# Top-32 attention with two expert layers on one core: the folds of the top-k read half of the scores from PSUM, the scores lose their factor of 1/8, and the order list is new

## The chip, the cores and the metric

One NeuronCore of a Trainium2 chip runs the whole program. The metric is the device time of one execution in microseconds (us). The kernel before was run three times.

## The reference

```python
def _attn_ref(q, k, v):                      # 2 batches, 8 heads, 576 rows, head size 64
    scores = (1.0 / np.sqrt(64)) * np.matmul(q, k.transpose(0, 1, 3, 2))
    kth = np.partition(scores, -32, axis=-1)[..., -32:-31]
    scores = np.where(scores >= kth, scores, -1e9)
    attn = np.exp(scores - np.max(scores, axis=-1, keepdims=True))
    attn = attn / (np.sum(attn, axis=-1, keepdims=True) + 1e-09)
    return np.matmul(attn, v)

def reference(...):
    x = attention output as (1152 tokens, 512)
    h = x @ w_in                             # 512 -> 2048
    x = (h * np.cos(h)) @ w_out              # 2048 -> 512
    # top-1 routing to 8 experts of width 1024 with capacity 288: relu(x @ w1[e]) @ w2[e], times the gate
```

All inputs and outputs are fp32. The softmax of each row of scores keeps the 32 largest of 576 values.

## The kernel before

**Attention.** The work is cut into 36 steps. 32 of them (kind "n", called whole steps here) take 128 query rows of one batch for a pair of heads; four of them (kind "s", steps 16, 17, 20 and 22) take the 64 rows left over in a batch for four heads. A step has 2 x 576 scores on each of the 128 partitions, `Sp[128, 2, 576]`. `scores(s, i)` computes them in two parts. Each part is four small matmuls into the PSUM tile `S` (two banks, one buffer in all), which ScalarE or VectorE then copies to `Sp` (`evict`, L820, profile lines L664 and L665) with a factor of 1/8. In a whole step, part i is column half i of both heads; in the other four, part i is both column halves of one pair of heads. `Sp` has four buffers.

**Top-k.** `pair_chain(s)` runs on VectorE (DVE). Two folds (L834) write the elementwise maximum of the two column halves of `Sp` into the first half of `C`, and the minimum into the second half. Then three rounds of `max` (the eight largest of 288, L839) and `match_replace` (L842) follow for each of two heads, and one `max` over all 576 columns of `C` (L846). `C` has a single buffer, so the folds of step s+1 come behind the chain of step s. `softmax(s)` then makes the threshold and the maximum into two biases (L873, on GpSimd, called POOL in the profile; `factors` holds the two factors), subtracts a penalty from all scores below the threshold (L880 on ScalarE, L884 on POOL or DVE), takes the exponential (L887) and divides by the sum (L897 to L899). `products(s)` transposes the result on TensorE (L914), evicts the transposed parts `PT` (L664 or L665) and multiplies by v (L928 to L943).

**What runs beside it.** While attention runs, the weights of the first layer arrive and are converted (`convert`, L691 to L711) and split in two (`split_w`, `split_wo`: `rounded` and `subtract`). As soon as a tile of 128 tokens is complete, `layer_in`, `cosine`, `product` and `layer_out` compute the first layer for it, and `route` and `place` send it to its expert. After the last tile the experts follow one behind the other.

**What sets the order.** Every operation is entered into a `Plan` with its engine, a cost and the tiles that it reads and writes. `PICKS` chooses the engine of each operation that could run on two or three (`flex`): one digit for each, in the order in which they are entered. `ORDER` lists the numbers of all operations; `in_order` takes them by that list, as soon as what they depend on has been issued, and issues each to its engine's queue. The queue of an engine runs strictly in that order, so a wait at its head holds all that is behind it. The cost numbers of the plan only choose which buffer of a ring is taken; they are no times of the chip.

The lines that the change touches:

```python
evict(0.53, 0.67, copy, r=[kp], w=[("Sp", s, i)], scale=0.125)                      # L820
DVE.tensor_tensor(out=T["C", s][:, :, c:c + HS], in0=x[:, :, 0:HS], in1=x[:, :, HS:S], op=op)   # L834
```

Of the kernel before, what the change touches and what calls it, by code (L numbers as in the profile page):

```python
# [19 lines left out]
HS = S // 2  # L20
# [26 lines left out]
    "1000000000010000000000000000000000000001000000000000000001000000000000000000000000000000000001001100"  # L47
    "1010000001100000010000000001010100000001000000000000000001100000000100000000000000000001001000010001"
    "0001000100002000000000000000002000000012000001000000000020000000000000000000000000000000000002000100"
    "1100110001111010111110110000000010000000000000000000000000010000001000010100100001001011110101000101"  # L50
    "0101111010000000010100000101010000000100000000000001010010111000010000000000000000000011010010010010"
    "0001010001100100000000001000001101011111101001000010001100000000000001010000001000000000111101001000"
    "000000000100")
ORDER = [
# [489 lines left out]
def forward(ctx, lasting, tc, kq, vn, vs_, w_in, w_out, w_gate, w1, w2, out, paired):  # L544
# [250 lines left out]
    def scores(s, i):  # L795
# [19 lines left out]
        def copy():  # L815
            x = T["Sp", s]
            o = x[:, :, i * HS:(i + 1) * HS] if kind == "n" else x[:, i, :].rearrange("p (a c) -> p a c", c=HS)
            return o, T[kp][:, :, 0:HS]
        P.op("pe", 0.595 if kind == "n" else 1.025, mm, r=[k], w=[kp], tiling="rows" if kind == "n" else "quarters")
        evict(0.53, 0.67, copy, r=[kp], w=[("Sp", s, i)], scale=0.125)  # L820

    def chain(s):
        if paired:
# [822 lines left out]
```

## Time and profile before

| | us |
|---|---|
| median of 3 runs (lowest, highest) | 654.29 (653.79, 655.72) |
| the profiled execution, time | 652.3 |
| the profiled execution, span from first to last instruction | 650.4 |
| busy in the span: TensorE (PE) | 580.4 |
| VectorE (DVE) | 556.5 |
| ScalarE (ACT) | 499.0 |
| GpSimd (POOL) | 311.2 |

A share of 89% for TensorE over the whole span hides that the stages differ: attention with its conversions fills the first 200 us, attention and the first layer share the next 200, the rest of the first layer runs to about 465 us, and the experts fill what remains. So the busy time has to be read by stretches.

### The profile page before, as it was taken

To read this page: it belongs to the slowest core of one execution; us is meant where nothing else is said; L and a number is where in the kernel's file an instruction comes from. 1 tells how busy PE (TensorE), PEld (TensorE's weight loads), DVE (VectorE), ACT (ScalarE), POOL (GpSimd) and SP (SyncE) were. 2 spreads that over 40 slices of the span, in tenths; PEclk is the share of its full clock that TensorE was granted. 3 is DMA by queue.
4 is the path that set the end of the run, shared out by engine and by line. 5 is a ranking of instruction groups with operands and counts; after the bars stand their busy time and mean duration, and the time that the engine had idled before them with its cause. 6 is when DMAs were issued, how large, how long until landed. Compare 5 with 4: busy or idle time off the path is not lost.

```text
span 650.4 us, 11538 instructions
## 1 busy us (share of the span) xinstructions
PE 580.4 (89%) x3808; PEld 452.7 (70%) x3808; DVE 556.5 (86%) x1542; ACT 499.0 (77%) x1026; POOL 311.2 (48%) x367
## 2 busy tenths in 40 slices
PE   3456589787989999999999999999979999999994
PEld 1234476565545876778767788788679898889893
DVE  6999999999999999999999989555666787878782
ACT  3688799989998978889998986636635777678771
POOL 2466776755875777854776633434341121010111
PEclk9986699898999999999999999999969999999998
DMA  8656597722252222233212210124444696668650
GB/s 290 228 172 210 162 389 282 236 88 62 60 146 84 85 79 83 66 104 99 74 44 66 78 42 18 66 98 145 148 147 145 221 292 206 203 214 269 222 181 17
DMA packets 44613, 94.62 MB, mean 145 GB/s; under 512 B 7165, under 2 KB 11261, under 8 KB 44544
## 3 DMA queue, kind: packets, MB, share of 16 engines
q1 hardware_dynamic: 42800, 89.04, 41.9%
q0 software_dynamic: 1744, 4.76, 2.0%
q8 instruction: 32, 0.52, 0.3%
q14 instruction: 37, 0.30, 0.1%
HBM read 81.87 MB, written 12.69 MB: 145 GB/s over the span
## 4 chain that ended last, share of the span: by engine, by line
PE 40%; DVE 33%; ACT 11%; issue 11%; DMA 2%; POOL 2%; SPq 0%; POOLq 0%; DVEq 0%; ACTq 0%
DVE C L842 8%; PE yp L1495 7%; DVE W L839 7%; DVE C L834 5%; PE x L1101 5%; PE hp L1450 4%; PE x L1093 4%; DVE W L846 3%; PE hp L1455 2%; ACT Sp L897 2%; PE av L928 2%; PE pt L914 2%; PE h L1013 2%; PE h L1018 2%; ACT Sp L887 2%
## 5 line engine op out<-in xcount | busy, mean ns | idle before, releaser
L884 POOL TENSOR_TENSOR Sp<-Sp,pen 128x576 f32<-128x576 f32 x60 | 81.7, 1362 | 42.9 <-ACT pen L880 39.7
L842 DVE MATCH_REPLACE8 C<-W,C 128x288 f32<-128x288 f32 x216 | 94.4, 441 | 0.0
L839 DVE MAX8 W<-C 128x8 f32<-128x288 f32 x216 | 92.7, 449 | 1.5
L1500 POOL DMA_INDIRECT out_dram<-ot,ti x16 | 18.9, 1179 | 136.9 <-DVE ot L1514 55.0
L914 PE MATMUL pt<-ident,Sp 128*128 128x128 f32 x324 | 54.7, 295 | 26.4 <-ACT Sp L897 21.2
L806 PE MATMUL S<-kq 64*128 64x288 f32 x256 | 57.6, 532 | 21.6 <-ACT Sp L664 12.2
L914 PEld LDWEIGHTS pt<-ident,Sp 128*128 128x128 f32 x324 | 38.6, 148 | 51.1 <-ACT Sp L897 29.4
L1093 PE MATMUL x<-wo,hs 128*128 128x512 f32 x148 | 72.5, 602 | 1.6 <-POOL wo L711 0.9
L834 DVE TENSOR_TENSOR C<-Sp 128x576 f32<-128x576 f32 x72 | 64.3, 899 | 1.2
L880 ACT ACTIVATE pen<-Sp,tb 128x576 bf16<-128x576 f32 x72 | 55.5, 771 | 8.6 <-POOL tb L873 4.4
L887 ACT ACTIVATE Sp<-Sp,tb 128x576 f32<-128x576 f32 x72 | 55.6, 773 | 5.2 <-DVE Sp L884 3.1
L1020 PE MATMUL h<-xh,wl 128*128 128x256 f32 x192 | 54.1, 282 | 0.0
L806 PEld LDWEIGHTS S<-kq 64*128 64x128 f32 x256 | 22.7, 216 | 43.7 <-ACT Sp L664 21.9
L928 PEld LDWEIGHTS av<-PT,v 128*64 128x64 f32 x320 | 38.5, 150 | 20.6 <-ACT ws L705 6.5
L928 PE MATMUL av<-PT,v 128*64 128x128 f32 x320 | 47.4, 301 | 6.0 <-DMA v<-in_vn_dram 2.9
L846 DVE MAX8 W<-C 128x8 f32<-128x576 f32 x72 | 52.3, 747 | 0.4
L664 ACT ACTIVATE PT<-pt 128x384 f32<-128x384 f32 x98 | 46.1, 486 | 6.8 <-PE pt L914 6.3
L897 ACT ACTIVATE Sp<-Sp,sm 128x576 f32<-128x576 f32 x55 | 41.0, 771 | 11.2 <-DVE sm L892 11.2
L930 PE MATMUL av<-PT,v 128*64 128x128 f32 x320 | 47.2, 301 | 0.3 <-ACT PT L664 0.3
L664 ACT ACTIVATE Sp<-S 128x576 f32<-128x576 f32 x62 | 40.1, 647 | 9.4 <-PE S L806 6.3
L1077 POOL TENSOR_TENSOR hs<-hs,ur 128x512 f32<-128x512 f32 x27 | 35.3, 1308 | 16.7 <-ACT ur L1068 16.6
L1455 PE MATMUL hp<-xgs,la 128*128 128x192 f32 (+2 forms) x160 | 39.8, 252 | 0.0
(224 smaller groups left out, 1863.0 us busy)
## 6 DMA issues: line engine op xcount, KB each, us to landing
raw<-in_w_dram SPq DMA_DIRECT2D x64, 512.0 KB, 4.5
kq<-in_kq_dram SPq DMA_DIRECT2D x40, 288.0 KB, 2.9
v<-in_vn_dram SPq DMA_DIRECT2D x32, 320.0 KB, 3.5
wraw<-in_w_in_dram SPq DMA_DIRECT2D x16, 512.0 KB, 4.7
wraw<-in_w_out_dram SPq DMA_DIRECT2D x16, 512.0 KB, 6.2
xs<-z SPq DMA_DIRECT2D x1, 4680.0 KB
v<-in_vs_dram SPq DMA_DIRECT2D x8, 320.0 KB
out_dram<-z SPq DMA_DIRECT2D x1, 2304.0 KB
```

Source lines behind the costliest of these rows:

```text
L664: P.flex([("act", act, lambda: ACT.activation(*args(), AF.Copy, scale=scale), False), ("dve", dve, lambda: DVE.tensor_scalar(*args(), scal ...
L806: PE.matmul(T[kp][:, a, 0:HS], t[p, S:S + 128], t[p, i * HS:(i + 1) * HS], start=True, stop=True)
L834: DVE.tensor_tensor(out=T["C", s][:, :, c:c + HS], in0=x[:, :, 0:HS], in1=x[:, :, HS:S], op=op)
L839: P.op("dve", 0.372, lambda r=r, i=i: DVE.max(T["W", s][:, i, LIST[r]:LIST[r] + 8], T["C", s][:, i, 0:HS]), r=[("C", s, i)], w=[("W", s, i)])
L842: P.op("dve", 0.42, lambda r=r, i=i: DVE.match_replace(T["C", s][:, i, 0:HS], T["W", s][:, i, LIST[r]:LIST[r] + 8], T["C", s][:, i, 0:HS], ...
L846: P.op("dve", 0.665, lambda i=i: DVE.max(T["W", s][:, i, 40:48], T["C", s][:, i, :]), r=[("C", s, i), ("C", s, 2)], w=[("W", s, i)])
L880: P.op("act", 0.67, lambda i=i, kp=kp: ACT.activation(T[kp], T["Sp", s][:, i, :], AF.Relu, scale=-BIG, bias=T["tb", s][:, i, 0:1]), r=[ks, ...
L884: eng.tensor_tensor(out=T["Sp", s][:, i, :], in0=T["Sp", s][:, i, :], in1=T[kp], op=OP.subtract)
L887: P.op("act", 0.76, lambda i=i: ACT.activation(T["Sp", s][:, i, :], T["Sp", s][:, i, :], AF.Exp, bias=T["tb", s][:, i, 1:2], accum_out=T[" ...
L914: PE.transpose(T[kp][:, c * 128:(c + 1) * 128], P2[:, cc * 128:(cc + 1) * 128], ident)
L928: PE.matmul(o[0:64, 0:128], v[:, c * 64:(c + 1) * 64], chunk(c), start=(c == 0), stop=(c == 4), skip_group_check=True)
L1093: P.op("pe", 0.87, lambda f=f, a=a: PE.matmul(T["x2", t], T[kh][:, a:a + 128], T["wo", f], start=(f == 0), stop=(f == 15)), r=[kh, ("wo", ...
```

## The change

The factor of 1/8 is taken out of the eviction of the scores. It moves into the exponential, whose scale becomes 0.125, and into the factor of the maximum's bias (-0.125 for -1). The folds take their second operand, the other column half, from the PSUM tile `S` instead of from `Sp`. In a whole step the two folds read part 1 of the scores in PSUM, both heads at once (128x576). In the other four steps there are four folds of 128x288, two for each part. So the folds no longer depend on the eviction of part 1, and part 1 stays in the single buffer of `S` until the folds and the eviction have read it. The last `max` depends on its own half of the minima alone. One cost of the plan changes (0.70 to 0.74), and `PICKS` and `ORDER` are new.

```
-                                    POOL.memset(factors[:, 1:2], -1.0)), w=[("halfpi",)])
+                                    POOL.memset(factors[:, 1:2], -0.125)), w=[("halfpi",)])
...
-        evict(0.53, 0.67, copy, r=[kp], w=[("Sp", s, i)], scale=0.125)
+        evict(0.53, 0.67, copy, r=[kp], w=[("Sp", s, i)])
...
-        both = [("Sp", s, 0), ("Sp", s, 1)]
-        firsts = [("C", s, 0), ("C", s, 1)]
-
-        def halves(c, op):
-            x = T["Sp", s]
-            DVE.tensor_tensor(out=T["C", s][:, :, c:c + HS], in0=x[:, :, 0:HS], in1=x[:, :, HS:S], op=op)
-        for c, op, w in ((0, OP.max, firsts), (HS, OP.min, [("C", s, 2)])):
-            P.op("dve", 0.67, lambda c=c, op=op: halves(c, op), r=both, w=w, port=True)
+        whole = steps[s][0] == "n"
+
+        def fold(c, op, i):
+            x, o = T["Sp", s], T["C", s]
+            if whole:
+                DVE.tensor_tensor(out=o[:, :, c:c + HS], in0=T["S", (s, 1)][:, :, 0:HS], in1=x[:, :, 0:HS], op=op)
+            else:
+                DVE.tensor_tensor(out=o[:, i, c:c + HS], in0=T["S", (s, i)][:, 1, 0:HS], in1=x[:, i, 0:HS], op=op)
+        if whole:
+            for c, op, w in ((0, OP.max, [("C", s, 0), ("C", s, 1)]), (HS, OP.min, [("C", s, 2), ("C", s, 3)])):
+                P.op("dve", 0.69, lambda c=c, op=op: fold(c, op, 0), r=[("Sp", s, 0), ("S", (s, 1))], w=w, port=False)
+        else:
+            for i in range(2):
+                for c, op, w in ((0, OP.max, ("C", s, i)), (HS, OP.min, ("C", s, 2 + i))):
+                    P.op("dve", 0.40, lambda c=c, op=op, i=i: fold(c, op, i), r=[("Sp", s, i), ("S", (s, i))], w=[w], port=False)
...
-                T["Sp", s][:, i, :], T["Sp", s][:, i, :], AF.Exp, bias=T["tb", s][:, i, 1:2],
+                T["Sp", s][:, i, :], T["Sp", s][:, i, :], AF.Exp, bias=T["tb", s][:, i, 1:2], scale=0.125,
...
-            P.op("pe", 0.70, mm, r=[gh, gl, ("vh", f), ("vl", f)], w=[("x2", t)])
+            P.op("pe", 0.74, mm, r=[gh, gl, ("vh", f), ("vl", f)], w=[("x2", t)])
```

What the new `PICKS` say, counted by reading its digits in the order in which the operations are entered (before -> after, up to the end of the first layer):

| operation | ACT | DVE | POOL |
|---|---|---|---|
| eviction of scores | 62 -> 66 | 10 -> 6 | |
| eviction of `PT` | 98 -> 89 | 10 -> 19 | |
| eviction of `h` | 31 -> 29 | 1 -> 3 | |
| penalty (L884) | | 12 -> 10 | 60 -> 62 |
| division (L897 to L899) | 55 -> 49 | 12 -> 10 | 5 -> 13 |
| scaling in `convert` (L691) | 31 -> 25 | | 1 -> 7 |
| `rounded` of w_in, w_out, gh | 31 -> 24 | | 13 -> 20 |
| `subtract` of the same | | 21 -> 13 | 23 -> 31 |
| clamp (L1047) | | 11 -> 8 | 25 -> 28 |
| product with the cosine (L1077) | | 9 -> 12 | 27 -> 24 |

In the weights of the first two experts, four more `rounded` and four more `subtract` go to POOL. What the new `ORDER` says of the tile `S`, read the same way: in 9 of the 32 whole steps the eviction of part 1 is issued before the two folds, in 15 between them, and in 8 behind both. In three of those 15 steps DVE has no other operation between the two folds, in twelve it has one or more.

## Rows read from the trace of the kernel before

**Rows 1.** Busy time by stretch: length, then busy us (instructions) of each engine, clock

```profile
core 0: us, PE busy (x) PEld busy (x) DVE busy (x) ACT busy (x) POOL busy (x), PEclk, DMA share, GB/s
0.00:200.00 200.00, 145.85 (x908) 94.34 (x909) 191.22 (x498) 169.02 (x318) 127.35 (x146) 0.91 0.57 190
200.00:400.00 200.00, 196.94 (x1434) 150.92 (x1433) 191.98 (x542) 174.36 (x331) 130.01 (x166) 1.00 0.24 72
400.00:465.00 65.00, 64.91 (x457) 53.16 (x457) 40.08 (x115) 37.21 (x70) 27.04 (x32) 1.00 0.29 98
465.00:650.40 185.40, 172.66 (x1016) 154.25 (x1014) 133.19 (x390) 118.41 (x309) 26.75 (x24) 0.96 0.59 193
```

**Rows 2.** Waits in 20 to 200 us: engine, line, releaser; us in total, times, longest

```profile
PE pt L914 <- ACT Sp L897: 20.3, 9, 6.8
```

**Rows 3.** DVE groups: line, operation, shapes, count; busy us, mean ns; idle before

```profile
L842 DVE MATCH_REPLACE8 C<-W,C 128x288 f32<-128x288 f32 x216 | 94.4, 441 | 0.0
L839 DVE MAX8 W<-C 128x8 f32<-128x288 f32 x216 | 92.7, 449 | 1.5
L834 DVE TENSOR_TENSOR C<-Sp 128x576 f32<-128x576 f32 x72 | 64.3, 899 | 1.2
L846 DVE MAX8 W<-C 128x8 f32<-128x576 f32 x72 | 52.3, 747 | 0.4
```

**Rows 4.** The folds' own line: durations min/median/max in ns, first and last start

```profile
L834 DVE TENSOR_TENSOR C<-Sp x72: 732/749/1827, 9.9 to 391.1; 128x576 f32<-128x576 f32 x72
```

**Rows 5.** Busy time of the folds alone, by stretch

```profile
0.00:200.00 200.00, 28.61 (x34) 0.91 0.57 190
200.00:395.00 195.00, 35.71 (x38) 1.00 0.24 74
```

**Rows 6.** Timeline of one slow fold: start us, us, engine, line, operation

```profile
65.42 1.28 POOL L884 TENSOR_TENSOR Sp<-Sp,pen 128x576 f32<-128x576 f32 x1
65.66 1.65 DVE L834 TENSOR_TENSOR C<-Sp 128x576 f32<-128x576 f32 x1
```

**Rows 7.** DVE instructions with an input in PSUM (first: min/median/max; others: groups)

```profile
L665 DVE TENSOR_SCALAR Sp<-S x10: 736/742/759, 5.3 to 388.2; 128x576 f32<-128x576 f32 x10
...
L1460 DVE TENSOR_TENSOR ht<-hp,ht 128x192 f32<-128x192 f32 x56 | 19.2, 351 | 9.2 <-ACT ht L1459 9.0
L1460 DVE TENSOR_TENSOR ht<-hp,ht 128x128 f32<-128x128 f32 x8 | 2.1, 286 | 2.7 <-ACT ht L1459 2.7
```

**Rows 8.** DVE groups whose counts the new picks change

```profile
L884 DVE TENSOR_TENSOR Sp<-Sp,pen 128x576 f32<-128x576 f32 x12 | 10.1, 838 | 1.1 <-ACT pen L880 1.1
L1077 DVE TENSOR_TENSOR hs<-hs,ur 128x512 f32<-128x512 f32 x9 | 8.6, 960 | 2.0 <-ACT ur L1068 1.9
L898 DVE TENSOR_SCALAR Sp<-Sp,sm 128x576 f32<-128x576 f32 x12 | 7.9, 673 | 0.2
L1047 DVE TENSOR_SCALAR ur<-hs 128x512 f32<-128x512 f32 x11 | 6.3, 581 | 0.3 <-ACT hs L664 0.2
L665 DVE TENSOR_SCALAR PT<-pt 128x384 f32<-128x384 f32 x10 | 5.5, 547 | 0.7 <-PE pt L914 0.7
L655 DVE TENSOR_TENSOR wl<-ws,wh 128x512 fp32r<-128x512 f32 x4 | 2.7, 674 | 0.0
L665 DVE TENSOR_SCALAR hs<-h 128x512 f32<-128x512 f32 x1 | 0.7, 684 | 0.0
```

**Rows 9.** Groups of ACT and POOL: the eviction of the scores, the penalty, the division

```profile
L664 ACT ACTIVATE Sp<-S 128x576 f32<-128x576 f32 x62 | 40.1, 647 | 9.4 <-PE S L806 6.3 <-PE pt L914 2.7 <-PE S L812 0.3
L884 POOL TENSOR_TENSOR Sp<-Sp,pen 128x576 f32<-128x576 f32 x60 | 81.7, 1362 | 42.9 <-ACT pen L880 39.7 <-PE pt L914 2.5
L899 POOL TENSOR_TENSOR Sp<-Sp,sm 128x576 f32<-128x576 f32 x5 | 6.1, 1213 | 1.7 <-DVE sm L892 1.7
```

**Rows 10.** Timeline of two hand-overs, DVE to ACT and ACT to PE

```profile
70.39 0.14 DVE L892 RECIPROCAL sm<-sm 128x2 f32<-128x2 f32 x1
...
70.56 1.44 ACT L897 ACTIVATE Sp<-Sp,sm 128x576 f32<-128x576 f32 x2 [1.43 <-DVE sm L892]
...
72.06 0.47 PE L914 MATMUL pt<-ident,Sp 128*128 128x128 f32 x1 [6.83 <-ACT Sp L897]
```

**Rows 11.** Timeline of four matmuls of one part of the scores

```profile
63.89 1.33 PE L806 MATMUL S<-kq 64*128 64x288 f32 x4
```

More of the change, by code (lines that the diff above doesn't have):

```diff
@@ L46 @@
 PICKS = (
[L47 to L53, printed above, removed]
-ORDER = [
[185 rows of a table removed]
+    "1000000000000000000000000000000010000000000000000200000000000000000000000000000110000100000001000100"
+    "0010000000010000000000000100000000010100000000000100000002000000000210000000001001000010000000100000"
+    "0000000000000000000022000100000110000002000000022000000022010000001000000010000001122000000010000101"
+    "0011110001201110111111110000001010010000010000000101100000000000000000000010110101111101110100100101"
+    "0101100000000111011101111101010000001000000000000000100110110111010000000110000000101001001000011011"
+    "0001010000010101001011100100100110001111111101001010000000000101101000000010110101110011110110010001"
+    "000000000000")
+ORDER = [
[186 rows of a table added]
 ]
@@ L845, in pair_chain @@
         for i in range(2):
-            P.op("dve", 0.665, lambda i=i: DVE.max(T["W", s][:, i, 40:48], T["C", s][:, i, :]), r=[("C", s, i), ("C", s, 2)],
-                 w=[("W", s, i)])
+            P.op("dve", 0.665, lambda i=i: DVE.max(T["W", s][:, i, 40:48], T["C", s][:, i, :]),
+                 r=[("C", s, i), ("C", s, 2 + i)], w=[("W", s, i)])
     def full_chain(s):
```

371 rows, old and new, of the table ORDER are left out of this document.

## Prediction

> **What bounds the kernel now.** I read the busy time by stretches first, since the share over the whole span mixes stages. In the first 200 us VectorE (DVE) is busy for 191 us, ScalarE (ACT) for 169 us and TensorE (PE) for only 146 us. From 200 to 400 us DVE has 192 us and PE 197 us, and from 400 to 465 us PE has no gap left [rows 1]. So DVE sets the pace for 200 us, both share it for the next 200 us, and from there on PE has a backlog that it works off. The waits confirm the first part: the longest wait of PE in that time, 20.3 us, is for ACT's division, the end of a softmax that waits for DVE's chain [rows 2]. The groups of DVE say what it does: the top-k lines sum to 304 us, and none of them stood idle for more than 1.5 us before its instructions [rows 3]. DVE is never short of scores.
>
> The folds differ from their neighbours. They take 0.749 us in the median and 0.732 us at best, but 1.83 us at worst and 0.899 us in the mean [rows 3, 4]. The timeline shows a slow one: it starts while POOL subtracts a penalty, and ends some 0.6 us after POOL is done, so that nearly all of its surplus lies beside POOL's instruction [rows 6]. All 72 folds lose 64.3 - 72 x 0.749 = 10.4 us in this way. Only 28.6 - 34 x 0.749 = 3.1 us of it falls in the first 200 us [rows 5], where DVE alone sets the pace.
>
> **The change part by part.** *The fold itself.* A DVE instruction with one input in PSUM shows no such spread: the eviction of 128x576 takes 0.736 to 0.759 us over ten instances, beside a POOL that is busy for two thirds of the time [rows 1, 7]. A tensor-tensor operation with one input in PSUM takes 0.286 us for 128 columns and 0.351 us for 192, so 1.02 ns for each column, which makes 0.351 + 384 x 0.00102 = 0.74 us for 576 [rows 7]. I take 0.745 us; the bounds are 0.73 and 0.76. Whole steps: 64 x (0.899 - 0.745) = 9.9 us less DVE time. The other four steps trade 8 folds of 0.899 us for 16 of 0.351 + 96 x 0.00102 = 0.45 us, which is nothing.
>
> [...]
>
> *The factor of 1/8.* Eviction, bias and exponential keep their number and sizes; a scale of an instruction that already has one or can take one costs nothing, bounded by the 0.647 us of the eviction, which already carries the factor [rows 9].
>
> *The new picks.* Until the end of the chain of step 17 (before, this was at about 197 us) the new list gives DVE 3 evictions of scores, 2 products, 3 clamps, 3 penalties and 5 subtractions fewer, and 1 division, 2 evictions of `PT` and 1 of `h` more. By the rows: -2.2 - 1.9 - 1.7 - 2.5 - 3.4 + 0.7 + 1.1 + 0.7 = -9.2 us [rows 7, 8]. The means of penalty, product, division and clamp hold waits beside POOL, which more POOL work brings back, so I take -7. Over the whole first layer it is only -4.0 us (4 x 0.742 + 2 x 0.838 + 2 x 0.673 + 8 x 0.674 + 3 x 0.581 - 9 x 0.547 - 2 x 0.684 - 3 x 0.960), as later steps get the evictions. ACT loses 26 instructions, at most 26 x 0.647 = 17 us [rows 9], which it can use at 169 of 200 us [rows 1]. POOL gains 31, at up to 1.36 us each 42 us at most, on 257 us in 400 us [rows 1, 9]; it stays below 80%, and its cover is that a step's softmax may lag by several steps, with four buffers of `Sp`.
>
> *The new hold on `S`.* Part 1 now stays in the one buffer until the folds have read it, so PE's scores of step s+1, and all that is queued on PE behind them, wait for the folds of step s; before, they waited for an eviction only. From there to the folds of s+1, DVE has the chain, 6 x (0.449 + 0.441) + 2 x 0.747 = 6.8 us [rows 3]. In that time PE and ACT need two parts and an eviction: at most 2 x 1.33 + 0.65 us plus hand-overs, 3.5 us [rows 9, 11]. A hand-over takes 0.03 to 0.06 us (70.53 to 70.56, 72.00 to 72.06) [rows 10]. So 3 us of slack hide this hold, if PE is not behind by more than that; it is no longer hidden by scores made steps ahead, and each us beyond the slack is one of DVE's.
>
> *The two readers of part 1.* ACT's eviction and DVE's folds now read the same PSUM tile. No row of before shows two engines reading one PSUM tile without an order between them. I assume that the reads are put one behind the other, in the order of issue. In the 15 whole steps where the eviction is issued between the folds, ACT then waits for the first fold, and the second fold, with all of DVE behind it, waits for ACT: 0.65 us and two hand-overs, 0.75 us, less what DVE has between the folds. With ACT free at once this leaves 0.75 us in three steps and 0 to 0.4 us in the others, some 3.5 us in all, 2 of it in the 8 such steps of the first 200 us; the bounds are 0 (the reads need no order) and 15 x 0.75 = 11 us. I take 3 us in the first 200 us, as ACT has a queue.
>
> **The sum.** At 200 us DVE is ahead by 10.1 us (folds 3.1, picks 7) less 3 us of waits, so by 7 us, and PE, with 54 us of gaps there, can follow. From 200 to 465 us PE has 465 - 200 - 196.9 - 64.9 = 3.2 us of gaps [rows 1]: what DVE saves there, another 7 us on the folds less some 3 us that the picks give back and 3 us of waits, has nowhere to go. For PE waiting at `S` I take off 1 us. That leaves 6 us. The experts (185 us) are the same work. So the span goes from 650.4 to 644.4 us; the profiled execution took 1.9 us more than its span, and the median of the runs is 2.0 us above the profiled execution: 648.3 us. With 0 to 8 us of waits instead of 3, and a PE that loses 0 to 2 us, the forecast's own range is 643.5 to 652.
>
> **The rivals.**
> *More gain.* No waits, and PE also closes its 3.2 us after 200 us: 10.1 + 3.2 = 13 us, 641 us. For it: three engines are relieved where two of them are full. Against: the 15 interleaved steps.
> *Nothing.* The gaps of PE before 200 us are those of a start that waits for conversions and softmax latencies, and PE is the bound after it. What DVE saves becomes idle time: 652.5 to 656. For it: most of the fold's surplus lies after 200 us [rows 5]. Against: DVE's 191 of 200 us.
> *The fold costs what it did.* If an input in PSUM costs more than rows 7 say, the folds save 5 us less, only some 1 us of it before 200 us; or the eviction delays every fold as before. That ends near 651.
> *Slower.* The hand-over of `S` decides: the second fold waits for ACT, the next scores wait for both, and the slack of the steps doesn't hold because DVE, PE and ACT are all nearly full. At 0.75 us for each of the 32 whole steps this costs 24 us, against 14.4 us that DVE saves over the layer (10.4 + 4.0): 9.6 us slower, 664 us. It decides from 14.4 / 32 = 0.45 us a whole step on. For it: 15 interleaved steps, and a list that shows no room for it in three of them. Against: 3 us of slack a step, and in 9 steps the eviction comes first, as it always did. [...]
>
> **How the numbers follow.** A measurement of this kernel can tell some 0.3% from no change, 2 us: faster is below 652.3, slower above 656.3. Forecast 0.47, more gain 0.13, nothing 0.16, the same fold 0.04, slower 0.20. Faster: 0.47 + 0.13 + 0.03 of the others = 0.63; same 0.16; slower 0.21. The range goes from 641 to 660: below lie 0.06 of the gain, above about half of the slower case and more.
>
> **What would show it.** Right: folds of 0.74 to 0.76 us with no long ones; DVE 10 to 17 us less busy before 465 us; waits of DVE's folds for ACT's eviction of 2 to 6 us in all; the first fold of step 18 at about 190 us; PE as full as before from there. Wrong: waits of the folds above 12 us, waits of PE's scores for the folds above 5 us, or PE gaps after 200 us. The prediction fails if the new list brings waits between other engines that no count of instructions shows.

## The result and the profile after

The changed kernel takes 664.16 us (median of 4 runs, 662.63 to 665.48) against 654.62 us for the kernel before on the same chip: a ratio of 1.0144, interval 1.0117 to 1.0171. That is 9.4 us slower (0.0144 x 655), where 6 us faster had been forecast. Below, "over before" is always such a ratio less 1, times 655 us, since each group of runs has its own runs of the kernel before (medians 654.6 to 655.6). The profiled execution has a span of 662.4 us, 12.0 us more than before, as the profiled execution of the kernel before, 652.3 us, lies 2.3 us below that median.

The busy time by stretches of the kernel after; it answers to [rows 1]:

```profile
core 0: us, PE busy (x) PEld busy (x) DVE busy (x) ACT busy (x) POOL busy (x), PEclk, DMA share, GB/s
0.00:200.00 200.00, 143.25 (x917) 92.91 (x918) 187.29 (x495) 163.34 (x307) 132.42 (x169) 0.93 0.56 186
200.00:400.00 200.00, 194.01 (x1393) 146.38 (x1392) 189.74 (x540) 167.60 (x315) 128.44 (x171) 1.00 0.25 77
400.00:465.00 65.00, 64.67 (x467) 53.99 (x466) 40.95 (x107) 32.95 (x63) 25.12 (x34) 1.00 0.26 89
```

Every busy share before 400 us is lower except POOL's in the first row. DVE is 5.3 us less busy until 465 us (423.3 to 418.0), ACT some 17 us less, and PE has done 5.5 us less by 400 us: three relieved engines and a longer run, so they wait for one another.

Cut at the same piece of work, the end of the last chain and the end of the first layer (its last matmul), the kernel before, then the kernel after:

```profile
0.00:406.30 406.30, 349.09 (x2395) 250.70 (x2396) 389.28 (x1058) 347.25 (x655) 259.77 (x313) 0.96 0.40 130
406.30:470.60 64.30, 64.21 (x426) 52.08 (x424) 37.08 (x101) 35.44 (x66) 24.64 (x30) 1.00 0.33 110
```

```profile
0.00:406.90 406.90, 344.16 (x2371) 245.56 (x2373) 382.79 (x1054) 335.26 (x629) 263.87 (x343) 0.97 0.40 129
406.90:480.70 73.80, 70.01 (x453) 55.48 (x448) 44.07 (x103) 32.78 (x63) 30.82 (x40) 0.98 0.30 104
```

The last chain ends only 0.6 us later: DVE has 6.5 us less work up to there, and 7.1 us more idle time. The layer ends 10.1 us later, and by PE: it stood idle for 62.7 instead of 57.2 us up to the last chain, and for 3.8 instead of 0.1 us behind it.

The groups of DVE, by shape (operation, shapes, count; busy us, mean ns; idle before). The first two answer to [rows 3, 4], the rest to [rows 8]:

```profile
L835 DVE TENSOR_TENSOR C<-S,Sp 128x576 f32<-128x576 f32 x64 | 47.5, 750 | 6.4 <-ACT Sp L665 4.4 <-PE S L807 0.3
L837 DVE TENSOR_TENSOR C<-S,Sp 128x288 f32<-128x288 f32 x16 | 6.8, 449 | 0.6 <-ACT Sp L665 0.4
...
L709 DVE SCALAR_TENSOR_TENSOR wt<-wraw,wt 128x512 int32<-128x512 int32 x29 | 23.2, 810 | 0.0
...
L892 DVE TENSOR_TENSOR Sp<-Sp,pen 128x576 f32<-128x576 f32 x10 | 10.5, 1052 | 0.7 <-ACT pen L888 0.7
L906 DVE TENSOR_SCALAR Sp<-Sp,sm 128x576 f32<-128x576 f32 x10 | 9.5, 950 | 0.1
L656 DVE TENSOR_TENSOR gl<-hs,gh 128x512 fp32r<-128x512 f32 x8 | 7.1, 886 | 5.0 <-POOL gh L661 3.2 <-ACT gh L660 1.8
```

The folds cost what was forecast, with no long ones left. Other operations of DVE got dearer: the penalty rose from 838 to 1052 ns, the division from 673 to 950 [rows 8]. The conversion, and the last subtraction, in the kernel before:

```profile
L708 DVE SCALAR_TENSOR_TENSOR wt<-wraw,wt 128x512 int32<-128x512 int32 x29 | 20.4, 714 | 0.0
L655 DVE TENSOR_TENSOR gl<-hs,gh 128x512 fp32r<-128x512 f32 x10 | 7.1, 715 | 0.8 <-ACT gh L659 0.7
```

Waits at the tile `S` in the whole span of the kernel after (engine, line, releaser: us, times, longest):

```profile
PE S L807 <- DVE C L835: 16.5, 4, 7.4
...
PE S L807 <- ACT Sp L665: 5.0, 6, 1.2
DVE C L835 <- ACT Sp L665: 4.4, 11, 0.7
...
ACT Sp L665 <- DVE C L835: 3.5, 6, 1.1
```

PE waits for the folds, and DVE and ACT take turns at part 1. The timeline shows the first at its longest. Scores from 10 us on, kernel before, then kernel after (start us, us, engine, line; in brackets the idle time before and what ended it):

```profile
13.10 1.33 PE L806 MATMUL S<-kq 64*128 64x288 f32 x4 [0.74 <-ACT Sp L664]
15.18 1.33 PE L806 MATMUL S<-kq 64*128 64x288 f32 x4 [0.75 <-ACT Sp L664]
```

```profile
14.83 1.33 PE L807 MATMUL S<-kq 64*128 64x288 f32 x4 [7.38 <-DVE C L835]
16.90 1.33 PE L807 MATMUL S<-kq 64*128 64x288 f32 x4 [0.74 <-ACT Sp L665]
25.45 1.33 PE L807 MATMUL S<-kq 64*128 64x288 f32 x4 [7.22 <-DVE C L835]
```

Before, PE ran ahead at the pace of the evictions; now it makes two parts and stands until the next folds. The same step 9, later in the run, before and after:

```profile
100.07 0.76 PE L806 MATMUL S<-kq 64*128 64x288 f32 x4
103.09 0.64 ACT L664 ACTIVATE Sp<-S 128x576 f32<-128x576 f32 x1
106.86 0.75 DVE L834 TENSOR_TENSOR C<-Sp 128x576 f32<-128x576 f32 x1
```

```profile
106.94 0.76 PE L807 MATMUL S<-kq 64*128 64x288 f32 x4
107.80 0.64 ACT L665 ACTIVATE Sp<-S 128x576 f32<-128x576 f32 x1
108.47 0.76 DVE L835 TENSOR_TENSOR C<-S,Sp 128x576 f32<-128x576 f32 x1 [0.45 <-ACT Sp L665]
```

The scores were done 106.86 - 100.83 = 6.0 us before their fold, now 108.47 - 107.70 = 0.8 us. Worked out in this way for the 31 whole steps from step 1 on (first fold's start less the modelled end of part 1's last matmul), the median of this lead fell from 6.0 to 1.0 us, and the steps with less than 1.9 us went from 2 to 21.

Near the end of the first layer a third thing shows. DVE, POOL and PE of the kernel after:

```profile
470.69 3.96 DVE L1237 TENSOR_TENSOR doubtb<-doubts 128x1 bf16<-128x1 f32 x1
474.58 0.68 DVE L1085 TENSOR_TENSOR hs<-hs,ur 128x512 f32<-128x512 f32 x1
...
470.87 3.77 POOL L657 TENSOR_TENSOR wl<-raw,wk 128x512 fp32r<-128x512 f32 x3
...
476.05 0.50 PE L1109 MATMUL x<-vh,gh 128*128 128x512 f32 x1 [2.98 <-ACT gh L660]
```

An addition of 128x1 takes 3.96 us beside three subtractions of POOL; behind it on DVE stands the product that PE's last matmuls need. After the 2.98 us in which PE stood, its granted clock, 1.00 until then, was 0.50 from 476.4 to 479.8 us, and its matmuls came 0.43 us apart instead of 0.23: some 1.6 us more for eight of them. (After 3.00 us in h2 it stayed at 1.00; and in the kernel before it was 0.50 from 475 to 485 us, behind 4.2 us in which PE's longest wait was 0.58 us.) Four us of these matmuls, and four us of them in the run f4 below, where PE did not wait so long:

```profile
476.00:480.00 4.00, 3.95 (x10) 2.90 (x11) 1.30 (x2) 0.00 (x0) 0.00 (x0) 0.57 0.36 123
```

```profile
474.00:478.00 4.00, 4.00 (x19) 3.21 (x18) 3.22 (x6) 0.63 (x1) 0.57 (x2) 1.00 0.26 67
```

The addition in the kernel before:

```profile
464.74 0.17 DVE L1229 TENSOR_TENSOR doubtb<-doubts 128x1 bf16<-128x1 f32 x1
```

The last matmul of the first layer ends at 480.7 us instead of 470.6 us (after, then before); what follows takes 181.7 and 179.8 us:

```profile
480.35 0.39 PE L1109 MATMUL x<-vh,gl 128*128 128x512 f32 x1
```

```profile
470.24 0.39 PE L1101 MATMUL x<-vh,gl 128*128 128x512 f32 x1
```

### The profile page after: what moved, and what is told of

It reads as the page before. It is cut to its first block, busy times and chain, and to the rows that moved or that the text cites. A ratio compares the mean times of both kernels' runs of the same rounds, so it can differ in the third digit from the quotient of the medians.

```text
span 662.4 us, 11583 instructions
## 1 busy us (share of the span) xinstructions
PE 583.6 (88%) x3808; PEld 452.8 (68%) x3808; DVE 557.3 (84%) x1541; ACT 484.3 (73%) x996; POOL 318.1 (48%) x406
## 4 chain that ended last, share of the span: by engine, by line
PE 41%; DVE 35%; issue 12%; ACT 6%; POOL 3%; DMA 1%; POOLq 0%; SPq 0%; DVEq 0%; ACTq 0%
DVE C L850 8%; DVE W L847 7%; PE yp L1503 6%; PE x L1109 5%; DVE C L835 4%; PE hp L1458 4%; PE x L1101 4%; DVE W L854 3%; PE h L1026 3%; DVE wt L709 3%; PE h L1028 2%; PE h L1027 2%; PE hp L1463 2%; PE av L936 2%; PE pt L922 2%
## 5 line engine op out<-in xcount | busy, mean ns | idle before, releaser
L807 PE MATMUL S<-kq 64*128 64x288 f32 x256 | 56.0, 519 | 33.4 <-DVE C L835 16.5
L1508 POOL DMA_INDIRECT out_dram<-ot,ti x16 | 16.1, 1004 | 140.1 <-ACT ot L1517 72.3
L1028 PE MATMUL h<-xh,wl 128*128 128x256 f32 x192 | 54.2, 282 | 0.0
L665 ACT ACTIVATE Sp<-S 128x576 f32<-128x576 f32 x66 | 42.3, 641 | 14.7 <-PE S L807 9.3
L835 DVE TENSOR_TENSOR C<-S,Sp 128x576 f32<-128x576 f32 x64 | 47.5, 750 | 6.4 <-ACT Sp L665 4.4
L665 ACT ACTIVATE PT<-pt 128x384 f32<-128x384 f32 x89 | 41.6, 488 | 13.7 <-PE pt L922 10.7
L936 PE MATMUL av<-PT,v 128*64 128x128 f32 x320 | 45.6, 291 | 5.5 <-DVE xl L969 4.0
L936 PEld LDWEIGHTS av<-PT,v 128*64 128x64 f32 x320 | 36.5, 144 | 17.9 <-DVE xl L969 5.5
L938 PE MATMUL av<-PT,v 128*64 128x128 f32 x320 | 45.6, 291 | 1.8 <-DVE PT L666 1.2
L905 ACT ACTIVATE Sp<-Sp,sm 128x576 f32<-128x576 f32 x49 | 37.0, 769 | 4.8 <-DVE sm L900 4.6
L1458 PE MATMUL hp<-xgs,wk 128*128 128x384 f32 x128 | 39.9, 374 | 0.0
```

What stands on the lines that cost most here:

```text
L665: P.flex([("act", act, lambda: ACT.activation(*args(), AF.Copy, scale=scale), False), ("dve", dve, lambda: DVE.tensor_scalar(*args(), scal ...
L807: PE.matmul(T[kp][:, a, 0:HS], t[p, S:S + 128], t[p, i * HS:(i + 1) * HS], start=True, stop=True)
L835: DVE.tensor_tensor(out=o[:, :, c:c + HS], in0=T["S", (s, 1)][:, :, 0:HS], in1=x[:, :, 0:HS], op=op)
L936: PE.matmul(o[0:64, 0:128], v[:, c * 64:(c + 1) * 64], chunk(c), start=(c == 0), stop=(c == 4), skip_group_check=True)
L1028: PE.matmul(o, lo, a, start=False, stop=(kc == 3), skip_group_check=True)
L1458: PE.matmul(o, hi_at(ka)[:, c:c + 128], x.rearrange("p a n -> p (a n)"), start=(kc == 0), stop=False, skip_group_check=True)
```

## The experiments

| run | us | ratio to before (95%) | over before, us |
|---|---|---|---|
| the change | 664.16 | 1.0144 (1.0117, 1.0171) | +9.4 |
| e1: folds from `S`, old lists | 729.97 | 1.1159 (1.1113, 1.1204) | +75.9 |
| e2: folds from `Sp`, new lists | 729.37 | 1.1144 (1.1100, 1.1188) | +74.9 |
| e3: eviction ahead of both folds | 670.68 | 1.0251 (1.0210, 1.0293) | +16.4 |
| e4: eviction behind both folds | 667.86 | 1.0189 (1.0144, 1.0234) | +12.4 |
| e5: new order, old picks | 671.71 | 1.0255 (1.0203, 1.0306) | +16.7 |
| f1: one reader of part 1 | 660.13 | 1.0074 (1.0050, 1.0098) | +4.8 |
| f4: three subtractions to DVE | 660.86 | 1.0079 (1.0050, 1.0108) | +5.2 |
| g4: f1 and f4 | 656.65 | 1.0023 (1.0001, 1.0045) | +1.5 |
| g1: before, shorter last maximum | 651.43 | 0.9937 (0.9905, 0.9968) | -4.1 |
| g2: after, shorter last maximum | 658.84 | 1.0051 (1.0030, 1.0073) | +3.3 |
| g3: factor of 1/8 alone | 654.27 | 0.9982 (0.9959, 1.0005) | -1.2 |
| h1: `S` held 0.8 us longer | 671.82 | 1.0234 (1.0185, 1.0284) | +15.3 |
| h2: no hold, new lists | 677.50 | 1.0365 (1.0330, 1.0400) | +23.9 |
| h3: h2 and a shorter last maximum | 665.22 | 1.0158 (1.0117, 1.0199) | +10.3 |
| h4: the folds of h2, old lists | 654.28 | 0.9976 (0.9952, 1.0001) | -1.6 |
| k1: h3, scores moved ahead | 735.24 | 1.1216 (1.1161, 1.1272) | +79.6 |
| k2: h4, scores moved back | 686.23 | 1.0475 (1.0439, 1.0512) | +31.1 |

The intervals reach 1.4 to 3.6 us to either side, so a difference of two rows is good to some 2 to 5 us.

**First question: the folds or the lists (e1, e2)?** e1 is the kernel after with the `PICKS` of before and its `ORDER`, 86 entries of it moved so that the scores of a step come behind the folds of the step before. e2 keeps the new lists:

```diff
-                DVE.tensor_tensor(out=o[:, :, c:c + HS], in0=T["S", (s, 1)][:, :, 0:HS], in1=x[:, :, 0:HS], op=op)
+                DVE.tensor_tensor(out=o[:, :, c:c + HS], in0=x[:, :, 0:HS], in1=x[:, :, HS:S], op=op)
```

> The changed kernel with the old PICKS and the old ORDER. The old list makes scores steps ahead, which the one buffer of S no longer allows: 86 of its entries (scores and their evictions) are moved to right behind the folds of the step before; in all 32 whole steps the eviction is issued ahead of the folds. Theory 1 (reading the folds from PSUM costs the time, by holding S and by ordering ACT and DVE): 659 us or more. Theory 2 (the new list and picks cost it, and the folds alone gain what they lose beside POOL): 648 to 653 us. Either way the folds take 0.745 us.

> The changed kernel with new PICKS and ORDER, but the folds read both halves from SBUF again, so that S is free after the eviction and ACT and DVE have no order on S. Theory 1 (PSUM read costs the time): 652 to 656 us, the waits of DVE's folds for ACT and of PE's scores for the folds go, the folds take 0.85 to 0.9 us again. Theory 2 (new list and picks): 663 to 668 us, since it loses the shorter folds and keeps the list.

Both came out at 729 to 730 us. By its letter e1 fits theory 1 ("659 us or more"), but e2, which takes the PSUM folds out, fits neither theory and is as slow. The longest waits at the scores, e1 first, then e2:

```profile
ACT Sp L663 <- PE S L805: 60.3, 36, 7.4
```

```profile
DVE C L835 <- ACT Sp L665: 38.6, 25, 3.4
```

Folds and lists can't be told apart by exchanging one of them: a list is made for one set of waits, and the new one has 23 of the 32 evictions of part 1 behind a fold that, in e2, must wait for them.

**Where the eviction stands between the folds (e3, e4).** In `ORDER`, the eviction of part 1 was moved in whole steps, here in step 5 (folds 228 and 229, eviction 227), in e3 and in e4:

```diff
-    164, 228, 201, 227, 169, 170, 229, 165,
+    164, 227, 228, 201, 169, 170, 229, 165,
```

```diff
-    164, 228, 201, 227, 169, 170, 229, 165,
+    164, 228, 201, 169, 170, 229, 227, 165,
```

> The changed kernel, with one edit of ORDER: in every whole step the eviction of part 1 is issued ahead of both folds (the change does so in 9 of 32). If the eviction between the folds is what costs time (4.4 us of DVE waits for it), 657 to 660 us. If not, 662 to 666 us.

> The changed kernel, with one edit of ORDER: in every whole step the eviction of part 1 is issued behind both folds. DVE then never waits for ACT at a fold of a whole step (4.4 us to 0), ACT waits for DVE and S is held longer. If DVE's waits for the eviction are the cause: 657 to 660 us. If the hold of S or ACT's queue counts more: 664 to 670 us. If the list as a whole is the cause: 662 to 666 us.

Both are dearer than the change's own mix, by 7.0 and 3.0 us, the second hardly clear of the noise. Neither place beats the one between the folds, so that place is not what costs.

**One reader (f1).**

```diff
-            return o, T[kp][:, :, 0:HS]
+            return o, x[:, :, 0:HS] if other else T[kp][:, :, 0:HS]
+        other = kind == "n" and i == 1
...
-        evict(0.53, 0.67, copy, r=[kp], w=[("Sp", s, i)])
+        evict(0.53, 0.67, copy, r=[("Sp", s, 0)] if other else [kp], w=[("Sp", s, i)])
```

> The changed kernel, but in the 32 whole steps the eviction of part 1 reads part 0 of Sp in SBUF instead of the PSUM tile S. So part 1 of S has one reader, the two folds, and neither engine waits for the other at it. Left out: part 1 of the scores never reaches Sp, so the softmax of these steps works on a copy of part 0; the top-k itself sees the right scores. Theory 'two readers' (ACT and DVE take turns at part 1 of S, and this is where the 10 us of the first layer go): 650 to 656 us, and the wait of DVE's folds for ACT's eviction (4.4 us) goes. Theory 'hold' (part 1 stays in the only buffer of S until the folds, whoever else reads it): 660 to 665 us.

4.6 us of the 9.4 went (4.0 by the medians). 660.1 us lies at the lower end of what the theory of the hold gave, and falls short of the 8 us or more that the theory of the two readers asked for: the second reader is a cause, not the whole. (In f1 the eviction doesn't wait for PE's part 1 either, but ACT's waits for scores fell from 9.3 to 7.7 us only.) The folds keep their 748 ns and no longer stand idle for ACT; the eviction from SBUF takes 675 ns:

```profile
L836 DVE TENSOR_TENSOR C<-S,Sp 128x576 f32<-128x576 f32 x64 | 47.1, 748 | 3.4 <-PE S L807 1.5
...
L665 ACT ACTIVATE Sp<-Sp 128x576 f32<-128x576 f32 x31 | 20.9, 675 | 0.0
```

A sibling of it (f2) freed `S` by folding part 0 with itself. Its values set off the kernel's own guard, which repeats the whole forward pass, so its 1438 us can't be compared (its trace has 640 matmuls of scores instead of 320); h2 stands in for it.

> The changed kernel with its lists, but the folds read part 0 of Sp in SBUF twice (add for the maximum, subtract for the minimum, same shapes), so that S is freed by its eviction alone, as in the kernel before, and the folds wait for no eviction of part 1. Left out: the folds never see part 1 of the scores, so the top-k picks other values. Theory 'hold': the waits of PE's scores for the folds (16 us) go; the folds lose some 10 us to POOL again, as in the kernel before; 647 to 656 us. Theory 'two readers': 650 to 656 us too, so this run does not tell these two apart, the run without the second reader does. Theory 'the list alone' (the order and the engines chosen are worse whatever S does): 664 to 675 us.

**The port at the end (f4).** "The port" is short here for what VectorE and GpSimd lose when they work at the same time. Three digits of `PICKS` turn POOL's subtractions of the second expert's weights into DVE's:

```diff
-    "0001010000010101001011100100100110001111111101001010000000000101101000000010110101110011110110010001"
+    "0001010000010101001011100100100110001111111101001010000000000101101000000010110100100010110110010001"
```

> The changed kernel, but three subtractions of the second expert's weights that GpSimd runs one behind the other at 470.9 us go to VectorE (three digits of PICKS from 1 to 0). Nothing is left out. In the trace a 128x1 operation of VectorE took 3.96 us beside these three, against 0.165 us in the kernel before, and TensorE then stood 2.98 us. Theory 'port at the end': this gap closes, 660.5 to 662.5 us. Theory 'the experts wait for something else': 664 us, no change.

4.2 us less (3.3 by the medians), and the addition is short again:

```profile
473.67 0.21 DVE L1237 TENSOR_TENSOR doubtb<-doubts 128x1 bf16<-128x1 f32 x1
```

**Both at once (g4).**

> The changed kernel with both edits that made it faster: the eviction of part 1 reads part 0 of Sp in SBUF (part 1 of the scores is left out of the softmax), and three subtractions of the second expert's weights go to VectorE. If the two causes are independent their 4.0 and 3.3 us add: 656 to 658 us, and about 2 us stay between this and the kernel before. If both edits only shift the same wait: 659 to 661 us.

7.9 us of the 9.4 are gone, against 8.8 for the two apart, so the two causes are nearly independent, and g4 ends 1.5 us (0.1 to 2.9) above the kernel before.

**The picks (e5)** and **the factor alone (g3)**: `PICKS` of the kernel before in the kernel after; and, in the kernel before,

```diff
-        evict(0.53, 0.67, copy, r=[kp], w=[("Sp", s, i)], scale=0.125)
+        evict(0.53, 0.67, copy, r=[kp], w=[("Sp", s, i)])
```

with the factor in the exponential and the bias, as in the change.

> The changed kernel with its order, but with the engines of the kernel before (PICKS of the kernel before). Nothing is left out. [...] Theory 'order and engines belong together': above 670 us, with engines waiting for one another in many places.

> The kernel before with one part of the change alone: the factor of 1/8 leaves the eviction and goes into the exponential and the bias. Nothing is left out. All theories: 653.5 to 656.5 us, no change; a difference of over 2 us would mean that a term put at nothing is not nothing.

The new picks are worth 7.3 us in the new order, although they load POOL; so more work on GpSimd is out as the cause of the loss, and e5 lies where the theory put it, if barely. The factor costs nothing that shows: -1.2 us in g3, and the eviction by ACT takes 647 ns before and 641 after, the exponential 773 and 771.

**What is a microsecond of DVE worth (g1 in the kernel before, g2 in the kernel after)?**

```diff
-DVE.max(T["W", s][:, i, 40:48], T["C", s][:, i, :])
+DVE.max(T["W", s][:, i, 40:48], T["C", s][:, i, 0:432])
```

> The kernel before, but the last maximum of each chain looks at 432 of the 576 columns of C. Left out: half of the minima, so that the 32nd value can come out a little lower. It takes about half-way between the maxima of 288 and 576 columns, so some 0.15 us less, 72 x 0.15 = 10.8 us of VectorE's time, spread evenly over the steps, and nothing else changes. It prices what VectorE's time is worth to the end of the kernel. Theory 'half of it' (what the prediction assumed: VectorE sets the pace until 200 us, TensorE after that): 5 us less, 649 to 651 us. Theory 'nothing' (TensorE's gaps before 200 us are latencies): 654 to 656 us. Theory 'all of it': 644 to 646 us.

> The changed kernel with the same shorter last maximum (432 of 576 columns; half of the minima are left out), 10.8 us less of VectorE's time. Theory 'half of it': 658 to 660 us. Theory 'nothing' (the scores and the evictions set the pace now, through the one buffer of S): 663 to 665 us. Theory 'all of it' (VectorE holds S, and so everything, in each step): 653 to 655 us.

The maximum took 597 ns instead of 747 in g1:

```profile
L846 DVE MAX8 W<-C 128x8 f32<-128x432 f32 x72 | 41.5, 597 | 0.4
```

Of these 10.8 us, 4.1 reach the end of the kernel before (38%) and 6.1 that of the kernel after (56%). By the intervals each share may be some 20 points off, so that the two don't differ for certain.

**Has the hold on `S` slack (h1)?** `late` is true in whole steps, in the first round, for the second head:

```diff
+                    if late:
+                        DVE.tensor_copy(T["W", s][:, 1, 0:1], T["S", (s, 1)][:, 0, 0:1])
...
+                P.op("dve", 0.372, eight, r=[("C", s, i)] + ([("S", (s, 1))] if late else []), w=[("W", s, i)])
```

> The changed kernel, but in the 32 whole steps VectorE reads one more column of part 1 of S (128x1, into an unused place of W) behind the first two maxima of the chain. Nothing is left out. S is held some 0.8 us longer in each whole step, and VectorE has 32 x 0.07 = 2.2 us more work, worth about 1 us at the end by the run with the shorter last maximum. Theory 'slack' (the prediction: some 3 us of slack a step hide the hold): 665 to 667 us. Theory 'no slack' (the scores of the next step come just in time for its folds, since they can't be made ahead any more): about 20 steps have under 1 us between scores and fold and lose 0.8 us each, 16 us of VectorE's time, at 0.5 to 1 us each: 673 to 681 us.

5.9 us more than the change (7.7 by the medians). The copies took twice what was expected, 32 x 0.14 = 4.5 us (the 0.07 us for each was the author's estimate), and explain 4.5 x 0.56 = 2.5 of it. That leaves some 3 us for 32 x 0.8 = 26 us of longer hold: neither "hidden" nor "each step pays". The waits of folds for evictions rose from 4.4 to 9.4 us:

```profile
PE S L807 <- DVE W L852: 19.0, 7, 8.0
...
DVE C L835 <- ACT Sp L665: 9.4, 12, 2.8
```

```profile
L852 DVE COPY W<-S 128x1 f32<-128x1 f32 x32 | 4.5, 140 | 0.0
```

**Without any hold (h2, h3, h4).** Folds of two heads of part 0, in SBUF, in the kernel after (h2), with a last maximum over 320 columns besides (h3), and in the kernel before with its own lists (h4):

```diff
-                DVE.tensor_tensor(out=o[:, :, c:c + HS], in0=T["S", (s, 1)][:, :, 0:HS], in1=x[:, :, 0:HS], op=op)
+                DVE.tensor_tensor(out=o[:, :, c:c + HS], in0=x[:, 0:1, 0:HS].to_broadcast([128, 2, HS]),
+                                  in1=x[:, 1:2, 0:HS].to_broadcast([128, 2, HS]), op=op)
```

> The changed kernel with its lists, but the folds of a whole step compare the two heads in part 0 of Sp, in SBUF (the other four steps fold their own part in SBUF), so that S is freed by its eviction alone and no fold waits for the eviction of part 1. Left out: the top-k of whole steps sees other values (part 0 of both heads). The folds then lose some 18 us beside GpSimd, worth 9 us at the price of the shorter last maximum. Theory 'the hold costs nothing': 670 to 676 us. Theory 'the hold costs 8 us or more': 656 to 666 us.

> As the kernel without the hold, but the last maximum looks at 320 of the 576 columns of C (most of the minima are left out too), which takes some 19 us off VectorE and so makes up for what its folds lose beside GpSimd. VectorE's work is then that of the changed kernel, and only the hold and the second reader of S are gone. The second reader alone was worth 4.0 us. Theory 'the hold costs nothing beyond that': 659 to 664 us. Theory 'the hold costs as much again or more': 648 to 656 us.

> The kernel before with its own lists, and the same folds as in the kernel without the hold: the two heads of part 0 of Sp in SBUF in whole steps, no wait for the eviction of part 1. Left out: the top-k of whole steps sees other values. Against the kernel without the hold it differs by the lists alone (and the four other steps). Theory 'the old folds never waited': 653 to 656 us. If the folds of the kernel before did wait for evictions: 645 to 651 us.

h2 and h4 have the same whole-step folds and nothing that holds `S`, and differ by 25.5 us: that is the price of the new lists when the folds read SBUF. (The trace of h2 is of its fastest execution, 672.6 us, and lies only 17.6 us behind that of h4.) Two parts of it can be named. The whole-step folds take 957 ns in h2 and 901 in h4, and the other four steps, which h2 folds in 16 instructions instead of 8, 12.0 against 8.3 us: 3.2 + 3.7 = 6.9 us of DVE, some 4 us at the end by g2's 56%. And the slow addition that f4 priced at 4.2 us is in the new picks, so h2 has it too, with 3.97 us.

```profile
L835 DVE TENSOR_TENSOR C<-Sp 128x576 f32<-128x576 f32 x64 | 60.5, 957 | 1.2
...
L838 DVE TENSOR_TENSOR C<-Sp 128x288 f32<-128x288 f32 x16 | 12.0, 776 | 0.2
```

```profile
L835 DVE TENSOR_TENSOR C<-Sp 128x576 f32<-128x576 f32 x64 | 57.3, 901 | 0.7
...
L838 DVE TENSOR_TENSOR C<-Sp 128x576 f32<-128x576 f32 x8 | 8.3, 1038 | 0.0
```

From h2 to the change it is 14.5 us back: the gain of the PSUM folds, net of the hold and of the second reader. So the balance is -1.6 (h4) + 25.5 (lists) - 14.5 (folds) = +9.4 us. It adds up runs, and is no list of causes: the lists cost 25.5 us with folds in SBUF, while with folds in PSUM the new lists are 66.5 us faster than the old ones as moved in e1. And h3, where DVE has the work of the change (425.7 against 426.9 us until the end of the first layer) and `S` is free, is no faster than the change. That doesn't show that the hold costs nothing: POOL is busy for 325.9 us until then in h3 and for 294.7 in the change, so its operations pay for folds in SBUF too. The leads are 5.6 us in h4, but 1.7 us in h2 and 0.8 us in h3, where nothing but the list makes the scores late. Yet the folds of h2 hardly wait (1.2 + 0.2 us in the rows above), so it isn't there that a short lead is paid.

**Run-ahead given back or taken away (k1, k2).** In `ORDER`, the scores and evictions of a step were moved: in k1 up, towards the chain two steps before (163 entries); in k2 down, behind the folds of the step before (79 entries). Of step 8 in k2, the scores of part 0 are operation 353 and go behind the second fold of step 7, to place 463 of the list:

```diff
-place 415: 353
+place 463: 353
```

> The kernel without the hold and with the short last maximum (665.2 us), and in its order list 163 entries moved: scores, evictions and the loads of kq of each step from 2 on stand nearly one step earlier (scores of part 0 in the middle of the chain two steps before), as the tile S now allows. The same parts of the top-k are left out as there. Theory 'run-ahead' (the new list costs time because scores come just in time): the 21 of 31 whole steps with under 1.9 us between scores and fold become few, and the time falls to 652 to 660 us. Theory 'something else in the list': 664 us or more; the move may also cost something where it pushes other work of TensorE and ScalarE back.

> The kernel before with folds that wait for no eviction of part 1 and hold no S (654.3 us; the top-k of whole steps sees other values), but 79 entries of its order list moved so that the scores of each step come behind the folds of the step before. S is free, only the list takes the run-ahead away. Theory 'run-ahead': 675 us or more, towards the 730 us of the old list with folds from S. Theory 'the hold and the second reader were what cost in that run': 654 to 662 us.

Neither settles it. k2 lost 32.7 us against h4, as the theory of the run-ahead asks; but k1, which should have won, lost 69 us against h3, with the longest median lead of all (8.1 us), and its DVE waits for something else altogether:

```profile
DVE xl L968 <- ACT xh L974: 33.4, 14, 8.7
```

Moving so many entries by rule can cost this much by itself, so k2 shows no more than k1.

## Why the prediction was wrong, point by point

**The fold's own price was right.** 0.750 us against 0.745, 0.449 against 0.45. With one input in PSUM a fold takes 0.750 us in the median, with both in SBUF 0.749 [rows 4]: no extra cost of PSUM shows at this size.

**"At 200 us DVE is ahead by 10.1 us less 3 us of waits, so by 7 us" failed.** This is the first step of the sum that went wrong. The first fold of step 18 was to start some 7 us earlier; it starts 0.7 us earlier, at 212.3 instead of 213.0 us. DVE's work up to there fell by 4.8 us instead of 10.1, and its idle time rose by 4.1 us (the rows are below).

**The term "14.4 us less DVE over the layer" was mis-sized.** It was 6.5 us up to the end of the last chain (5.3 us until 465 us). The folds gave their 64.3 - 47.5 - 6.8 = 10.0 us. The rest of DVE's work, put at 4.0 us less, took 3.5 us more: the step that failed priced the other operations over the layer at the means that they had before. Four groups alone rose by 29 x 0.096 + 10 x 0.214 + 10 x 0.277 + 8 x 0.171 = 9.1 us; elsewhere some is won. In h2, with the new lists but the folds back in SBUF, the first two of these groups are nearly as cheap as before, the third is not, and the subtraction stays at 886 ns:

```profile
L709 DVE SCALAR_TENSOR_TENSOR wt<-wraw,wt 128x512 int32<-128x512 int32 x29 | 21.1, 737 | 0.0
L907 DVE TENSOR_SCALAR Sp<-Sp,sm 128x576 f32<-128x576 f32 x10 | 10.0, 999 | 0.1
L893 DVE TENSOR_TENSOR Sp<-Sp,pen 128x576 f32<-128x576 f32 x10 | 8.4, 841 | 0.8 <-ACT pen L889 0.8
```

So, by this pair of runs, conversion and penalty (4.2 us of the 9.1) got dearer as the folds went out of POOL's way, and division and subtraction (4.1 us) by the new lists. Folds with one input in PSUM never took more than 0.759 us, those with both in SBUF up to 1.827 us [rows 4], and the 128x1 addition, with both inputs in SBUF, took 3.96 us beside POOL and 0.165 us in the kernel before.

**The picks were sized about right.** -7 us of DVE until step 17 was said. DVE's busy time until the end of that step, before, in e5 (new order and folds, old picks) and after:

```profile
0.00:212.90 212.90, 158.23 (x1007) 102.58 (x1007) 203.83 (x532) 179.86 (x340) 135.18 (x158) 0.92 0.56 186
```

```profile
0.00:220.20 220.20, 154.33 (x996) 100.75 (x997) 204.45 (x535) 179.34 (x339) 117.60 (x154) 0.92 0.54 175
```

```profile
0.00:212.20 212.20, 155.28 (x1010) 101.70 (x1011) 199.05 (x524) 173.54 (x328) 139.75 (x178) 0.94 0.55 182
```

From e5 to the change -5.4 us; from before to e5 +0.6 instead of the folds' -3.1. (The prediction put the end of step 17 at 197 us; it is at 212.9. The time read was that of step 16's second fold.)

**The waits of the two readers were sized about right, and their worth too low.** 3 us were said for the first 200 us. DVE's idle time until the end of step 17 rose from 9.1 to 13.1 us (212.90 - 203.83, 212.20 - 199.05), and in f1 it is 9.5 us. The waits of DVE's folds for ACT, 4.4 us, lie in the range of 2 to 6 us that was named; in the trace of f4, whose operations up to there are the same, they are 7.4 us. At the end the second reader was worth 4.6 us.

**"3 us of slack hide this hold" failed.** It compared the work of a step on PE and ACT (3.5 us) with the chain (6.8 us), as if both engines were free when `S` is. From 200 us on PE is nearly full with other work (197 of 200 us before), and the scores queue behind it: the median lead fell to 1.0 us, and h1 showed that a hold of 0.8 us more isn't hidden. "For PE waiting at `S` I take off 1 us" was mis-sized too: PE's scores waited 16.5 us for the folds, where more than 5 us was to be a sign of being wrong. Much of that took the place of other waits, as PE's idle time up to the last chain rose by 5.5 us only. The old kernel had a lead of 6.0 us, and the prediction noted its loss ("no longer hidden by scores made steps ahead") without a price; no run here prices it alone. The same operations in another list cost 25.5 us between h4 and h2. That a list can be so much dearer was not in the sum, which only counted instructions.

**"PE can follow" failed.** PE stood idle for 54.2 us in the first 200 us before [rows 1] and for 56.8 after, and for 6.0 instead of 3.1 us in the next 200. So the layer ended later although the chains ended at the same time. Even a clean gift of 10.8 us of DVE brings only 4.1 us to the end of the kernel before (g1): at 38%, 10 us would have given some 4, not 6, and the 6.5 us that DVE really saved some 2.5.

**One edit was left out of the sum.** Four `rounded` and four `subtract` in the experts' weights went to POOL, as the text ahead of the prediction says, and the prediction held that part for "the same work". Three of them held DVE for 3.96 us in front of PE's last matmuls: 4.2 us by f4, of which some 3 are PE's wait; the rest fits the 1.6 us at the lower clock after it. What comes behind the first layer did stay the same, 181.7 against 179.8 us.

**The rival "slower" hit the number, 664 us, by luck.** Its mechanism, 0.75 us in each of 32 steps at the second fold, would have shown 24 us of waits for ACT; the trace has 4.4, and f1 gives the second reader 4.6 of the 9.4 us.

**The range did not follow from its terms.** 0 to 8 us of waits instead of 3, and 0 to 2 us of PE instead of 1, make 644.3 to 654.3 us around the forecast, not 643.5 to 652.

**What stays open.** The second reader and the slow addition explain 7.9 of the 9.4 us (g4). Why the DVE time that was saved brought nothing on top is read from the traces, from DVE's idle time and PE's, and no run takes these waits away. What in the new lists costs 25.5 us in h2, beyond some 4 us at the folds and some 4 at the addition, is not shown. That the scores come just in time in them is measured; that this is the cost is not, since the folds of h2 hardly wait and k1 and k2 disturbed too much else. What the hold on `S` costs by itself is not shown either.

## What to carry to other kernels

Time that an instruction loses beside another engine isn't all saved by taking that instruction out of the way (here 10.0 us at the folds, with 4.2 us back at conversion and penalty): ask who meets the other engine next, and count what such a microsecond is worth at the end by shortening an instruction (g1), before building on it. If an edit lets a slow consumer hold a single buffer, look at the lead that its producer loses, as the trace shows it (consumer's start less producer's end, step by step), and not only at the length of the hold; but the lead is a sign and no price, as k1 shows. Compare two kernels at the same piece of work, not at the same time, to see which engine passes a delay on. When a change comes with new engine choices, cost all of them, the last ones before a stage's end above all.

## What the runs showed of the hardware

In the kernel after, a 128x1 VectorE operation waited out three GpSimd instructions in a row (3.96 us beside 3.77 us), not just the one that ran when it started; with them moved (f4) it took 0.21 us. PE's granted clock fell to 0.50 after it had stood 2.98 us there, and stayed at 1.00 in f4, where it had not; after 3.00 us in h2 it stayed at 1.00 too, so that no rule for it follows. And ScalarE and VectorE, reading one PSUM tile, took turns here, at up to 0.7 us a wait of VectorE and 1.1 us of ScalarE. These are waits at the program's own semaphores, and no run left them out.
